# Tail scores in 64x64 quarters of TensorE, without zero padding, with a new order and new banks

## The chip, the cores and the metric

One core of a Trainium2 chip runs the whole kernel. The metric is the device time of one execution in microseconds: the median of three runs before the change is 801.45 us (800.21 to 803.18). The profiled execution took 798.73 us, of which 796.7 us lie between its first and its last instruction.

## The reference

Two stages follow one another, both in fp32. Stage 1 is attention with a threshold for 8 batches, 8 heads, 576 rows and 64 columns of a head; stage 2 is a mixture of 4 attention experts on its output, each row of which uses the two with the largest gate.

```python
# stage 1, for each batch and head: q, k, v are [576, 64]
scores = scale * q @ k.T
thresh = max(scores, -1) - tau
scores = where(scores >= thresh, scores, -1e9)
attn   = softmax(scores);  x = attn @ v           # x: [576, 512], all heads side by side
# stage 2, for each batch
logits = x @ w_gate;  topk = the two largest of 4;  w = softmax over these two
for e in range(4):
    q, k, v = x @ wq[e], x @ wk[e], x @ wv[e]     # [576, 64]
    a = softmax(where(causal, -1e9, scale * q @ k.T))
    out += (e in topk) * w[e] * (a @ v @ wo[e])
```

## The kernel before, in words

576 rows are four tiles of 128 rows and a tail of 64. Heads (stage 1) and experts (stage 2) are taken two at a time, since a head has 64 columns: one lies in partitions 0 to 63, the other in 64 to 127 (`heads` names the two halves). A full tile's scores of two heads are two matmuls of 64 rows by 128 columns that work in the upper and the lower half of the array, each into its own bank.

A tail has 64 rows only, so two of them make one tile of 128 output partitions. In stage 1 `scores` (line 942) joins the tails of two neighbouring pairs n-1 and n: `qz0` and `qz1` (line 807) are [128, 128] tiles of zeros in which `prep` fills the 64 columns of the one or the other pair. For each half of the columns (`hf`, 288 each) the kernel runs, for each head half j, the matmul of `qz0` with the keys of pair n-1 and adds that of `qz1` with those of pair n: eight matmuls of 64x128, of which half the columns multiply zeros. That is done once for each odd pair, 16 times. In stage 2 `scores2` (line 1143) joins the tails of the two experts of a pair `ep`: `q2d0` and `q2d1` (line 810) are block-diagonal tiles [128, 128], filled by two copies on ACT at the end of `projected` (line 1094); two matmuls over the full array use them, 16 times in all (8 batches, 2 pairs of experts).

Every fp32 matmul stands in the trace as two passes, each a LDWEIGHTS and a MATMUL row; those of projections and outputs (tiles in fp32r) are one pass.

The order is not written in the loops. Every operation is first put on a list with an estimate of its time. `arrange` (line 340) then sends the list through a model of the five engines: among the operations that are ready it takes the one with the lowest rank, a number from the tables `PLACE` and `PLACE_OP`; `CHANGE` (line 130) is what the model adds on TensorE when a matmul uses the array in another shape than the one before. `loosen` (line 487) gives every accumulation its bank from the table `BANKS`. `fill` (line 503) puts bf16 matmuls on a constant tile `still` where the model sees TensorE idle; there are 146. The engines then run their lists in that order, each waiting for semaphores.

A batch of stage 2 (`moe`) runs mixed with the next batch's stage 1. PE runs the scores, the transposes and the products; DVE reads scores out of the banks with their minimum (line 742, the mask at line 737); ACT runs two passes over each score tile (lines 760 and 754); POOL scales; SP starts DMAs, among them transposes of fp16 tiles (`T<-hl`).

Of the kernel before, what the change touches and what calls it, by code (L numbers as in the profile page):

```python
# [64 lines left out]
    "ctload": 21.58207, "ctt0": 0.8201564, "ctt1": 1.191231, "cvload": 0.7750551, "cvx": 0.7924649, "cvy": 0.2206414,  # L65
# [8 lines left out]
    "dtload": -2.15, "dtt0": 0.8163344, "dtt1": 0.9896782, "dvload": 51.9424, "dvx": 0.6755247, "dvy": 0.919954,  # L74
# [11 lines left out]
    "ovload": -7.436486, "ovx": 0.7431236, "ovy": 0.9078734, "perm": 3.2453, "qT": -0.2869131, "qload": 0.3382297,  # L86
# [4 lines left out]
}  # L91
PLACE_OP = {
    "ACT gw": -194.9887, "ACT kx": 131.3286, "ACT lg": 32.86921, "ACT p2": -202.4545, "ACT pb": -91.43077,
    "ACT pp": 101.5619, "ACT pt2": -21.09828, "ACT q2": 32.05941, "ACT q2d0": -14.54573, "ACT q2d1": -45.12697,
    "ACT qi": 86.16288, "ACT qx": -46.57733, "ACT qz0": -111.7469, "ACT qz1": -45.9329, "ACT tau_t": 9.119313,
    "ACT tq": -0.2682498, "ACT v2": 41.76934, "ACT warm": 50.16119, "ACT wkh": 33.61568, "ACT woh": -31.10502,
    "ACT wqh": -8.614884, "ACT wvh": -61.59402, "ACT x": -7.572205, "ACT z0": 69.30023, "ACT z1": 72.23125,
    "ACT zt": 70.11606, "DVE col": -77.59164, "DVE gate": -76.59955, "DVE gt": 21.13243, "DVE gw": -10.09983,
# [28 lines left out]
PSUMS = "s", "g"  # L127
LAST_OUT = 3
KEYS_BY = "DVE", "ACT"
CHANGE = ((0, 160, 195, 115, 110), (218, 23, 201, 119, 25), (198, 163, 0, 20, 120), (225, 165, 80, 0, 145), (216, 25, 223, 150, 50))  # L130
EXP_SB = True
AV2_GROUPS = ((4, 3), (2, 1, 0))
T2_GROUPS = ((4,), (3,), (2,), (1, 0))
# [424 lines left out]
def kernel(  # L558
# [249 lines left out]
    for t in qz:  # L808
        memset("POOL", t, 0.0)
# [515 lines left out]
```

## Time and profile before

| | |
|---|---|
| median of three runs | 801.45 us |
| profiled execution / its span | 798.73 us / 796.7 us |
| PE busy | 774.5 us, 97% |
| DVE busy | 697.1 us, 87% |
| ACT busy | 671.3 us, 84% |
| POOL busy | 390.9 us, 49% |
| stage-1 tail scores on PE (`kx,qz`) | 256 passes, 34.7 us busy |
| stage-2 tail scores on PE (`q,q2d`) | 64 passes, 19.6 us busy |
| ACT copies into `q2d` | 32, 6.8 us |

Busy time of PE runs to the modelled end of each matmul, and passes overlap; how long a group holds the array is therefore read from the starts of neighbouring groups in the timeline, not from busy time. A shape such as `64*128` is rows by columns of the array that the pass uses.

### The profile page before, as it was taken

What the parts mean: (1) busy time and instruction counts of PE and PEld (TensorE: products, weight loads), DVE (VectorE), ACT (ScalarE), POOL (GpSimd) and SP (SyncE); (2) the same over time, 40 slices, a digit from 0 to 9 for tenths busy, and PEclk for the clock granted to TensorE, in tenths of its full rate; (3) what the DMA queues carried; (4) which work ended last, traced back from release to release, by engine and by line L of the source; (5) the groups of instructions that cost most, each with busy time, mean ns of one, the idle gap of its engine ahead of it and who ended that gap; (6) DMA issues with size and microseconds to landing.
All of it is one profiled execution on the core that took longest, in us unless ns stands there. A gap on an engine that the chain in (4) does not pass through costs nothing.

```text
span 796.7 us, 27639 instructions
## 1 busy us (share of the span) xinstructions
PE 774.5 (97%) x10802; PEld 641.5 (81%) x10802; DVE 697.1 (87%) x2124; ACT 671.3 (84%) x1766; POOL 390.9 (49%) x551
## 2 busy tenths in 40 slices
PE   8999999999999999999999899999999999999998
PEld 6778878788878887788887787878877888778986
DVE  3999899988999899989899898998899988998374
ACT  4898789997999969998899878999799996998364
POOL 5774346643647336553365533664355733656010
PEclk9999999999999999999999999999999999999999
DMA  7431476856677668784759556695767755756102
GB/s 166 98 84 42 103 146 113 158 102 133 123 160 144 114 110 157 164 138 96 147 112 190 97 112 136 129 191 103 134 119 158 132 115 102 150 109 115 28 28 81
DMA packets 319010, 96.37 MB, mean 121 GB/s; under 512 B 305696, under 2 KB 314144, under 8 KB 318880
## 3 DMA queue, kind: packets, MB, share of 16 engines
q1 hardware_dynamic: 317152, 94.21, 59.7%
q8 instruction: 85, 1.39, 0.7%
q10 hardware_dynamic: 1728, 0.39, 0.3%
q14 instruction: 45, 0.37, 0.1%
HBM read 31.47 MB, written 9.44 MB: 51 GB/s over the span
## 4 chain that ended last, share of the span: by engine, by line
PE 61%; DVE 21%; ACT 9%; DMA 4%; issue 3%; POOL 0%; SPq 0%; POOLq 0%; ACTq 0%; DVEq 0%
PE banks L645 54%; DVE pp L742 7%; PE banks L1294 6%; DVE hl L731 5%; ACT pp L760 3%; ACT pp L754 2%; DVE p L737 2%; DMA T<-hl 2%; DVE col L708 2%; PE banks L1291 1%; DMA ki<-in_k_dram 1%; ACT p L754 1%; DVE pt L682 1%; DVE x L731 1%; ACT pt L680 1%
## 5 line engine op out<-in xcount | busy, mean ns | idle before, releaser
L760 ACT ACTIVATE pp<-pp,col 128x576 f32<-128x576 f32 x286 | 211.8, 774 | 25.7 <-DVE col L708 21.3
L742 DVE TENSOR_SCALAR_CACHE_REDUCE pp<-banks 128x576 f32<-128x576 f32 x286 | 207.4, 748 | 18.3 <-PE banks L645 14.4
L708 POOL TENSOR_SCALAR hl<-pp,col 128x576 f16<-128x576 f32 x182 | 148.1, 825 | 140.9 <-ACT q L680 25.0
L754 ACT ACTIVATE pp<-pp 128x576 f32<-128x576 f32 x286 | 193.7, 681 | 0.5
L731 DVE SCALAR_TENSOR_TENSOR hl<-pp,col,hl 128x576 f16<-128x576 f32 x182 | 172.8, 959 | 14.1 <-POOL hl L708 14.0
L645 PE MATMUL banks<-kx,qx 64*128 64x288 f32 x1024 | 158.4, 425 | 1.4 <-DVE pp L742 0.7
L708 POOL TENSOR_SCALAR pp<-pp,col 128x576 f32<-128x576 f32 x104 | 80.5, 785 | 79.6 <-DVE col L720 35.0
L645 PEld LDWEIGHTS banks<-kx,qx 64*128 64x128 f32 x1024 | 93.6, 189 | 29.8 <-issue 6.9
L708 POOL TENSOR_SCALAR p<-p,col,gw 128x384 f32<-128x384 f32 (+3 forms) x115 | 89.0, 782 | 45.7 <-ACT p L754 23.1
L754 ACT ACTIVATE p<-p,col 128x128 f32<-128x128 f32 (+4 forms) x137 | 78.8, 581 | 16.5 <-DVE col L737 14.8
L645 PE MATMUL banks<-T,vh 128*64 128x128 f16 (+1 forms) x2940 | 85.5, 216 | 3.0 <-DMA T<-hl 2.6
L645 PEld LDWEIGHTS <-vh 128*64 128x64 f16 x2940 | 79.6, 110 | 10.2 <-issue 8.8
L737 DVE CUSTOM_DVE_ANT_0 p<-banks,mask 128x128 f32<-128x128 f32 (+4 forms) x137 | 66.0, 503 | 4.3 <-PE banks L645 3.1
L645 PE MATMUL banks<-wvh,x 128*128 128x260 f32 x320 | 64.3, 288 | 0.0
L680 ACT ACTIVATE pt<-banks 128x384 f32<-128x384 f32 (+2 forms) x128 | 58.7, 506 | 1.8 <-DVE pp L742 1.1
L645 PEld LDWEIGHTS banks<-wvh,x 128*128 128x128 f32 x320 | 51.4, 188 | 6.8 <-issue 5.5
L754 ACT ACTIVATION_READ_ACCUMULATOR pp<-pp 128x1 f32 x286 | 56.4, 197 | 0.0
L645 PE MATMUL banks<-x,wkh 128*128 128x288 f32 x256 | 53.9, 303 | 0.8 <-DVE pp L742 0.8
L645 PE MATMUL banks<-q,q 64*128 64x256 f32 (+3 forms) x256 | 52.8, 463 | 1.9 <-ACT pt L680 0.8
L645 PE MATMUL banks<-x,wqh 128*128 128x288 f32 x256 | 52.0, 296 | 0.0
L645 PE MATMUL banks<-pt,v 128*64 128x128 f32 (+1 forms) x960 | 51.3, 259 | 0.0
L645 PEld LDWEIGHTS banks<-pt,v 128*64 128x64 f32 x960 | 43.6, 137 | 7.9 <-issue 4.6
(147 smaller groups left out, 1619.5 us busy)
## 6 DMA issues: line engine op xcount, KB each, us to landing
ki<-in_k_dram SPq DMA_DIRECT2D x32, 256.0 KB, 3.7
vz<-in_v_dram SPq DMA_DIRECT2D x32, 256.0 KB, 2.9
qi<-in_q_dram SPq DMA_DIRECT2D x62, 128.0 KB, 2.7
out_dram<-st SPq DMA_DIRECT2D x30, 256.0 KB, 2.5
tk<-in_k_dram SPq DMA_DIRECT2D x16, 128.0 KB, 3.9
T<-hl SPq DMA_TRANSPOSE x91, 4.8
vz<-in_v_dram SPq DMA_DIRECT2D x64, 16.0 KB, 2.5
out_dram<-st SPq DMA_DIRECT2D x8, 128.0 KB, 2.4
```

Source lines behind the costliest of these rows:

```text
L645: lambda o, x, y: nc.tensor.matmul(o, x, y, start=start, stop=stop))
L680: run(e, t, [dst], [src], lambda d, s: nc.scalar.activation(d, s, AF.Copy))
L682: run(e, t, [dst], [src], lambda d, s: nc.vector.tensor_copy(d, s))
L708: return m.tensor_scalar(d, s, x_, y_, op0=op0, op1=op1)
L731: return nc.vector.scalar_tensor_tensor(d, a_, x_, r.pop(0), op0=op0, op1=op1, **kw)
L737: lambda o, a, i, m: nc.vector.tensor_tensor_reduce(o, i, m, 1.0, 3e38, ALU.add, ALU.min, a))
L742: lambda o, a, i: nc.vector.tensor_scalar(o, i, 1.0, None, op0=ALU.mult, op1=ALU.min, accum_out=a))
L754: return nc.scalar.activation(d, s, AF.Exp, scale=scale, **kw)
L760: lambda d, s, x: nc.scalar.activation(d, s, AF.Prelu, bias=x, scale=-1.0, alpha=1e36))
L1291: nc.tensor.matmul(banks[:, n, :256], still_[:, :P], still_[:, :1].to_broadcast([P, 256]), start=True, stop=True)
L1294: o.fn(*(r.place() for r in (*o.outs, *o.ins)))
```

## The change

The tail scores use quarters of the array. In stage 1 `qz0` and `qz1` become [128, 64] tiles without zeros; each of the eight matmuls is 64x64 and writes into the half of the partitions that belongs to its pair, so nothing is added up. In stage 2 the `q2d` tiles and their copies are gone; for each half of the columns two 64x64 matmuls read the last 64 columns of the query tile itself, one in the upper left and one in the lower right quarter, both into one bank, in different partitions. The model gets a sixth shape. All numbers of `PLACE`, `PLACE_OP` and `BANKS` are new, so the order on every engine is.

```diff
-    "LMo0": 86.31751, "LMo1": 37.79194, "LMo2": 39.95239, "LMo3": 4.177216, "LMo4": 4, "La00": 80.50161,
+    "LMo0": 82.11209, "LMo1": 57.35111, "LMo2": 36.64272, "LMo3": 17.42819, "LMo4": 4, "La00": 75.58571,
...
-CHANGE = ((0, 160, 195, 115, 110), (218, 23, 201, 119, 25), (198, 163, 0, 20, 120), (225, 165, 80, 0, 145), (216, 25, 223, 150, 50))
+CHANGE = ((0, 160, 195, 115, 110, 160), (218, 23, 201, 119, 25, 150), (198, 163, 0, 20, 120, 163), (225, 165, 80, 0, 145, 165),
+          (216, 25, 223, 150, 50, 150), (218, 150, 201, 119, 150, 23))
...
-    def matmul(o, x, y, start, stop):
+    def matmul(o, x, y, start, stop, share=4):
...
         if form:
-            t /= 4 if form == 4 else 2
+            t /= share if form == 4 else 2
...
-        plan.ops[-1].mode = 4 if form and x.dtype in HALF else form
+        plan.ops[-1].mode = 4 if form and x.dtype in HALF else 5 if form == 4 else form
...
-    qz = [const(f"qz{i}", [P, P]) for i in range(2)]
-    for t in qz:
-        memset("POOL", t, 0.0)
-    q2ds = [const(f"q2d{i}", [P, P]) for i in range(2)]
+    qz = [const(f"qz{i}", [P, ST]) for i in range(2)]
...
-        for t in q2ds:
-            memset("POOL", t, 0.0)
...
-                outs.append((qz[n % 2][:, heads[n % 2]], gs[0][:, R * D:(R + 1) * D]))
+                outs.append((qz[n % 2], gs[0][:, R * D:(R + 1) * D]))
...
-                    matmul(sp[j][:, hf, :HS], x[rows], y[rows, o:o + HS], i == 0, i == len(qks) - 1)
+                    to = sp[j][:, hf, :HS] if len(qks) == 1 else sp[j][heads[i], hf, :HS]
+                    matmul(to, x[rows], y[rows, o:o + HS], True, True)
...
-                if i == 0 and hf:
-                    for j, sl in enumerate(heads):
-                        copy("ACT", q2ds[ep][sl, j * ST:(j + 1) * ST], g[sl, SM - HS:HS])
...
-                matmul(g[:, hf, :HS], q2ds[ep], q2[1][:, cols], True, True)
+                for rows in heads:
+                    matmul(g[rows, hf, :HS], q2[0][rows, SM:], q2[1][rows, cols], True, True, 2)
```

Three places on PE follow. The first is a stage-1 tail after scores of stage 2 (`q,q` are query and key tiles of the experts, `kx` keys, `col,ones` a small sum, `woh,z` the output). Before:

```order
L1294 MATMUL banks<-ident,p_77 128x64 x4
L645 MATMUL banks<-q_100,q_101 128x384 x2
L645 MATMUL banks<-q_100,q_101 128x512 x2
L645 MATMUL banks<-kx_65,qz_180 128x288 x2
L645 MATMUL banks<-kx_66,qz_181 128x288 x2
L645 MATMUL banks<-kx_65,qz_180 128x288 x2
L645 MATMUL banks<-kx_66,qz_181 128x288 x2
L645 MATMUL banks<-col_116,ones 64x1 x2
L645 MATMUL banks<-woh,z_106 128x512
```

The same place in the changed kernel:

```order
L1290 MATMUL banks<-ident,p_76 128x64 x4
L647 MATMUL banks<-q_101,q_100 128x384 x2
L647 MATMUL banks<-q_101,q_100 128x512 x2
L647 MATMUL banks<-kx_65,qz_180 64x288 x2
L647 MATMUL banks<-kx_66,qz_181 64x288 x2
L647 MATMUL banks<-kx_65,qz_180 64x288 x2
L647 MATMUL banks<-kx_66,qz_181 64x288 x2
L647 MATMUL banks<-col_155,ones 64x1 x2
L647 MATMUL banks<-woh,z_106 128x512
```

Nothing has moved here; the eight matmuls now stand in another shape than the scores before them. The second place is a stage-1 tail among stage 2's value and key projections (`wvh`, `wvl`, `wkh` with `x`). Before:

```order
L645 MATMUL banks<-wvl,x_93 128x260
L645 MATMUL banks<-wvh,x_94 128x260
L645 MATMUL banks<-kx_65,qz_180 128x288 x2
L645 MATMUL banks<-kx_66,qz_181 128x288 x2
L645 MATMUL banks<-kx_65,qz_180 128x288 x2
L645 MATMUL banks<-kx_66,qz_181 128x288 x2
L645 MATMUL banks<-wvh,x_95 128x260
```

In the changed kernel:

```order
L647 MATMUL banks<-wvl,x_93 128x260
L647 MATMUL banks<-wvh,x_94 128x260
L647 MATMUL banks<-kx_65,qz_180 64x288 x2
L647 MATMUL banks<-kx_66,qz_181 64x288 x2
L647 MATMUL banks<-kx_65,qz_180 64x288 x2
L647 MATMUL banks<-kx_66,qz_181 64x288 x2
L647 MATMUL banks<-x_95,wkh 128x288
```

The tail is again between full-array matmuls; a projection of keys follows it in place of one of values. The third place is the second stage-2 tail of a batch (`ident,qi` and `ident,tq` are transposes of queries, `T,vh` the fp16 products of stage 1). Before:

```order
L1294 MATMUL banks<-ident,p_77 128x64 x16
L1294 MATMUL banks<-ident,qi_62 128x64 x8
L1294 MATMUL banks<-ident,tq_88 128x64
L645 MATMUL banks<-q_100,q2d_183 128x288 x2
L645 MATMUL banks<-woh,z_106 128x512
L645 MATMUL banks<-wol,z_106 128x512
```

In the changed kernel:

```order
L1290 MATMUL banks<-ident,p_77 128x64 x16
L647 MATMUL banks<-kx_65,qx_63 128x288 x4
L647 MATMUL banks<-q_101,q_100 64x288 x4
L647 LDWEIGHTS vh_74
L647 MATMUL banks<-T_84,vh_74 64x64
```

The tail has left its place in front of the full-array output matmuls and stands between scores in halves of the array and fp16 products.

## Rows read from the trace of the kernel before

**Rows 1.** The page, part 1: busy time, share of the span, instructions.
```profile
PE 774.5 (97%) x10802; PEld 641.5 (81%) x10802; DVE 697.1 (87%) x2124; ACT 671.3 (84%) x1766; POOL 390.9 (49%) x551
```
**Rows 2.** Windows: us of each engine's busy time, granted clock, DMA share, GB/s.
```profile
100.00:200.00 100.00, 98.84 (x1421) 82.48 (x1422) 92.61 (x282) 89.52 (x240) 50.96 (x70) 1.00 0.68 130
...
400.00:500.00 100.00, 95.95 (x1358) 78.86 (x1353) 91.53 (x279) 87.30 (x231) 51.74 (x68) 1.00 0.66 126
500.00:600.00 100.00, 99.08 (x1368) 82.32 (x1367) 91.39 (x279) 89.87 (x237) 51.89 (x70) 1.00 0.71 138
...
sum 600.00, PE 586.40 PEld 485.01 DVE 551.54 ACT 532.15 POOL 305.41; mean PE 97.73 PEld 80.84 DVE 91.92 ACT 88.69 POOL 50.90
```
**Rows 3.** The page, part 4: chain that ended last, shares by engine.
```profile
PE 61%; DVE 21%; ACT 9%; DMA 4%; issue 3%; POOL 0%; SPq 0%; POOLq 0%; ACTq 0%; DVEq 0%
```
**Rows 4.** What PE waited for: us in total, times, longest us.
```profile
PE banks L645 <- DMA T<-hl: 2.6, 3, 1.4
PE banks L1294 <- DVE st L682: 2.6, 5, 0.6
PE banks L645 <- DVE pp L742: 2.1, 5, 0.6
```
**Rows 5.** Groups by form: busy us, mean ns | idle before, releasers.
```profile
L645 PE MATMUL banks<-kx,qz 64*128 64x288 f32 x256 | 34.7, 409 | 0.0
...
L645 PE MATMUL banks<-q,q2d 128*128 128x288 f32 x64 | 19.6, 429 | 0.0
...
L680 ACT ACTIVATE q2d<-banks 64x64 f32<-64x64 f32 x32 | 6.8, 212 | 2.5 <-PE banks L645 2.3
```
**Rows 6.** PE's timeline, a stage-1 tail, whole and in narrow windows: start, us, count.
```profile
24.32 2.21 PE L645 MATMUL banks<-kx,qz 64*128 64x288 f32 x16
...
24.67 0.65 PE L645 MATMUL banks<-kx,qz 64*128 64x288 f32 x4
...
24.91 0.65 PE L645 MATMUL banks<-kx,qz 64*128 64x288 f32 x4
...
26.36 1.14 PE L645 MATMUL banks<-kx,qx 64*128 64x288 f32 x8
```
**Rows 7.** PE's timeline, 106 to 113 us: scores in halves, a stage-2 tail.
```profile
106.69 1.14 PE L645 MATMUL banks<-kx,qx 64*128 64x288 f32 x8
107.76 1.87 PE L645 MATMUL banks<-T,vh 128*64 128x128 f16 x60
109.55 1.24 PE L645 MATMUL banks<-kx,qx 64*128 64x288 f32 x8
...
111.03 1.24 PE L645 MATMUL banks<-q,q2d 128*128 128x288 f32 x4
112.11 0.38 PE L1291 MATMUL banks<-still 128*128 128x256 bf16 x2
```
**Rows 8.** PE's timeline: scores in halves between projections.
```profile
126.45 1.24 PE L645 MATMUL banks<-kx,qx 64*128 64x288 f32 x8
127.63 0.53 PE L645 MATMUL banks<-x,wqh 128*128 128x288 f32 x2
128.00 0.29 PE L645 MATMUL banks<-x,wql 128*128 128x288 f32 x1
```
**Rows 9.** PE's timeline: scores in halves between transposes.
```profile
170.88 1.19 PE L645 MATMUL banks<-kx,qx 64*128 64x288 f32 x8
171.91 0.22 PE L1294 MATMUL banks<-ident,ki 64*128 64x64 f32 x1
```
**Rows 10.** PE's timeline: products in column halves.
```profile
176.81 1.07 PE L645 MATMUL banks<-pt,vz 128*64 128x128 f32 x16
177.72 0.39 PE L645 MATMUL banks<-pb,vz 128*64 128x128 f32 x4
```

More of the change, by code (lines that the diff above doesn't have):

```diff
@@ L35 @@
     "F0": 0.2926676, "F1": 0.6107417, "F2": 0.7488845, "F3": 0.7924216, "Fv0": 0.7107417, "Fv1": 0.8924216,
[29 rows of a table removed]
-    "ctload": 21.58207, "ctt0": 0.8201564, "ctt1": 1.191231, "cvload": 0.7750551, "cvx": 0.7924649, "cvy": 0.2206414,
[8 rows of a table removed]
-    "dtload": -2.15, "dtt0": 0.8163344, "dtt1": 0.9896782, "dvload": 51.9424, "dvx": 0.6755247, "dvy": 0.919954,
[11 rows of a table removed]
-    "ovload": -7.436486, "ovx": 0.7431236, "ovy": 0.9078734, "perm": 3.2453, "qT": -0.2869131, "qload": 0.3382297,
[4 rows of a table removed]
[29 rows of a table added]
+    "ctload": 21.58207, "ctt0": 0.7700778, "ctt1": 1.137123, "cvload": -74.82518, "cvx": 0.7517662, "cvy": 0.6509301,
[8 rows of a table added]
@@ L91 @@
+    "dtload": -2.15, "dtt0": 1.023116, "dtt1": 1.286915, "dvload": 54.26096, "dvx": 0.6755247, "dvy": 0.919954,
[11 rows of a table added]
+    "ott1": 1.277065, "ovload": -14.41097, "ovx": 0.7858482, "ovy": 1.264367, "perm": 3.2453, "qT": -0.09700796,
[5 rows of a table added]
 }
 PLACE_OP = {
-    "ACT gw": -194.9887, "ACT kx": 131.3286, "ACT lg": 32.86921, "ACT p2": -202.4545, "ACT pb": -91.43077,
-    "ACT pp": 101.5619, "ACT pt2": -21.09828, "ACT q2": 32.05941, "ACT q2d0": -14.54573, "ACT q2d1": -45.12697,
-    "ACT qi": 86.16288, "ACT qx": -46.57733, "ACT qz0": -111.7469, "ACT qz1": -45.9329, "ACT tau_t": 9.119313,
@@ L96 @@
-    "ACT tq": -0.2682498, "ACT v2": 41.76934, "ACT warm": 50.16119, "ACT wkh": 33.61568, "ACT woh": -31.10502,
-    "ACT wqh": -8.614884, "ACT wvh": -61.59402, "ACT x": -7.572205, "ACT z0": 69.30023, "ACT z1": 72.23125,
-    "ACT zt": 70.11606, "DVE col": -77.59164, "DVE gate": -76.59955, "DVE gt": 21.13243, "DVE gw": -10.09983,
-    "DVE hl": 160.1341, "DVE kx": -3.048238, "DVE lg": 91.45051, "DVE p2": -37.58712, "DVE pa": -19.18527,
-    "DVE pp": -37.24325, "DVE qsc": 87.14683, "DVE st": -16.99811, "DVE still": 70.0155, "DVE tau_p": -56.81983,
@@ L101 @@
-    "DVE v2": -191.0278, "DVE vh": 55.56019, "DVE warm": -33.54305, "DVE x": 12.58504, "DVE z0": 72.70677,
-    "DVE z1": 54.42244, "DVE zt": 99.32354, "POOL col": -52.95213, "POOL gate": 12.7582, "POOL gt": -10.22238,
-    "POOL gw": -13.52735, "POOL hl": 33.24148, "POOL ident": 56.04437, "POOL mask": 198.4146, "POOL mask2": -34.26997,
-    "POOL ones": -34.48011, "POOL p2": 35.40006, "POOL pp": 7.380059, "POOL q2d0": 57.69175, "POOL q2d1": -251.2611,
-    "POOL qz0": -8.171826, "POOL qz1": -64.26274, "POOL st": -36.63575, "POOL tie": -109.6021, "POOL v2": -16.65763,
@@ L106 @@
-    "POOL vh": -2.22825, "POOL vz0": 9.108861, "POOL vz1": -42.16982, "POOL wkh": -18.74004, "POOL wkl": -38.99,
-    "POOL woh": -8.639636, "POOL wol": 51.72843, "POOL wqh": 6.561986, "POOL wql": 38.53265, "POOL wvh": 13.17268,
-    "POOL wvl": -20.27672, "SP T": -176.0207, "SP ki": -46.37165, "SP lg": -43.14256, "SP out": -201.4397,
-    "SP qi": 35.10716, "SP st": -110.6428, "SP tk": -57.4548, "SP tq": -97.81713, "SP vz0": -79.04153,
-    "SP vz1": 30.91814,
+    "ACT gw": -194.1128, "ACT kx": 114.9448, "ACT lg": 32.86921, "ACT p2": -220.9327, "ACT pb": -131.8278,
@@ new lines @@
+    "ACT pp": 94.57432, "ACT pt2": -0.9630147, "ACT q2": -22.7764, "ACT q2d0": -19.04289, "ACT q2d1": -63.05565,
+    "ACT qi": 88.63102, "ACT qx": -74.94887, "ACT qz0": -72.21189, "ACT qz1": -38.38221, "ACT tau_t": 42.36084,
+    "ACT tq": 36.34548, "ACT v2": 46.58959, "ACT warm": 35.37198, "ACT wkh": 33.61568, "ACT woh": -31.10502,
+    "ACT wqh": -8.614884, "ACT wvh": -61.59402, "ACT x": 5.80622, "ACT z0": 74.16211, "ACT z1": 84.51968,
+    "ACT zt": 72.79803, "DVE col": -54.82467, "DVE gate": -72.99998, "DVE gt": 48.00172, "DVE gw": -35.83652,
@@ new lines @@
+    "DVE hl": 124.0373, "DVE kx": 42.31811, "DVE lg": 91.45051, "DVE p2": -24.25269, "DVE pa": 6.372014,
+    "DVE pp": -3.043822, "DVE qsc": 114.638, "DVE st": -33.50564, "DVE still": 9.346285, "DVE tau_p": -35.47929,
+    "DVE v2": -154.8319, "DVE vh": 41.7296, "DVE warm": -36.33248, "DVE x": 36.36639, "DVE z0": 25.83054,
+    "DVE z1": 57.76388, "DVE zt": 50.61126, "POOL col": -52.95213, "POOL gate": 10.24712, "POOL gt": -11.96009,
+    "POOL gw": -14.24344, "POOL hl": 27.21407, "POOL ident": 42.55757, "POOL mask": 190.1404, "POOL mask2": -88.54509,
@@ new lines @@
+    "POOL ones": -92.00483, "POOL p2": 14.29299, "POOL pp": -25.7627, "POOL q2d0": 82.12945, "POOL q2d1": -277.5747,
+    "POOL qz0": -58.87586, "POOL qz1": -44.37684, "POOL st": -13.22116, "POOL tie": -66.38262, "POOL v2": -23.868,
+    "POOL vh": -59.47183, "POOL vz0": -2.888774, "POOL vz1": -83.19861, "POOL wkh": -36.14122, "POOL wkl": -5.395328,
+    "POOL woh": 12.84353, "POOL wol": 93.3955, "POOL wqh": 32.64844, "POOL wql": 23.29405, "POOL wvh": 16.25282,
+    "POOL wvl": -58.56358, "SP T": -247.5121, "SP ki": -49.72211, "SP lg": -8.129818, "SP out": -198.0919,
@@ L111 @@
+    "SP qi": 4.023193, "SP st": -108.2689, "SP tk": -38.2543, "SP tq": -91.20736, "SP vz0": -12.86307,
+    "SP vz1": 2.693464,
 }
@@ L115 @@
 BANKS = (
-    "50310220464001102347610453234502462404620103272126767535237620164602344535401050134512060462050412563410432067"
-    "13250130277454102774376056461766744705431770770266562016642702040562602267543246906420653456503F0B2463120761N4"
-    "622648134045436216321143062730055601327077454206351742512565005670765140563070166205637D5311D07075062ND5130624"
-    "6627327E698044K2304324G4G4GH7366274730541034424045733072610322101445216507772400312020743154075456731605621511"
-    "461600727746583513062431277631B314251741645202E2E1C3J512326014106532112556706660423722755430740323304606505050"
-    "5416472265014370213064M1463C0665437BL950206244132424505720761712654003034QI26107032675270060527467043601320516"
-    "5542076240320140612215303301553167277055154830F35207611069C950206246332120G098606A703571020202489A764742610456"
-    "13245177400676502307623453572266731015332232104716055642370612175425042960661037B12B0206244723614C15D365177751"
-    "3612662B2L55710435471072263315270075H015440423214065571543110235540240462335406601232716120625L0763236B853150H"
-    "5210744145041353J110623054090F0902051073416735055765504674B5410242340557626732025E176740702313041305756572"
+    "5401400426246732013327362754100206266J264510251077521064675430363Q03630367046036762512522525355712570157754267"
+    "6504760140342513101766701257215026M710426044340455272650607306023646462423640240906420616544322I407513320653E7"
+    "48L4ED2C03413667151277653055347326762371415540560677306110423015604576313132130757253H2A0636404560350625020624"
+    "70322744250464L72650160AB4G3P90122025460612303632704164266732670055436636732307O244576000332543737007665267023"
+    "C027304015751C950206246023720527625531373210502202I95746235371023767147014374666532104205414711730125454237270"
+    "34063716151005721260A19052C207064145095030624175265403144102257456P1L54G151B2004605344051124073462763646325151"
+    "44501755466004C412120043064172512041765303405130I607207351D530F06245543033403F503032407620G4535703214667203562"
+    "110527502462766423010354507062046047D206516640744516414155060764302A603040550737603K030624015271714G41B1454273"
+    "1BC901I7A4267303727053410171420356376375431004323121436037104276411405306740145737021354068404602052768I520406"
+    "423754670C11D05C227451253255009401551533423163625103004175K24020131551364751766708562024761636024775643740"
 )
```

101 rows, old and new, of the table PLACE are left out of this document.

## Prediction

> **What bounds the kernel now.** I read the busy shares first, then the busy time in windows, the chain that ended last, what PE waited for, and last the timeline around the two tails. PE is busy for 97% of the span [rows 1]. In the 600 us in the middle the windows give PE 97.7 us of each 100, DVE 91.9 and ACT 88.7, at the full clock (2.4 GHz) [rows 2]. PE is on the chain for 61%, DVE for 21%, ACT for 9% [rows 3]. The waits that PE is seen in are small: the longest entries are 2.6 us in total each [rows 4]. So PE's own work sets the time, with DVE 6 points behind it; a saving on PE should reach the end until DVE takes over.
>
> **The stage-1 tail.** A tail is 16 passes in the trace. They run in pairs, one pass in each half of the array: two starts of a pair are 0.24 us apart (24.67, then 24.91), and 16 passes hold PE from 24.32 to 26.36, which is 2.04 us [rows 6]. The first step there is longer (24.32 to 24.67, 0.35 us), so a change of shape into fp32 work costs about 0.11 on top of eight steps of 0.242. That a pair costs one step is seen against the full array: the tail over 128x128 takes four passes from 111.03 to 112.11, 1.08 us, and eight half passes take 1.07 from 106.69 to 107.76 [rows 7]. Column halves pair in the same way: 16 passes of 128 columns take 0.91 us from 176.81 to 177.72, eight steps of 0.11 (each fp32 pass takes about 2 cycles for a column) [rows 10]. Quarters, in which rows and columns are both halved, don't occur before. The bounds are these: four at a time, as both kinds of halves together suggest, and the eight passes of each half of the columns take two steps in place of four, so a tail takes four steps in place of eight; or only two at a time, and nothing is gained. I take four at a time, since both kinds of halves run at full pace. 16 tails x 4 steps x 0.242 = 15.5 us less on PE (other bound: 0).
>
> **The stage-2 tail.** Two full-array matmuls (four passes, four steps) become four quarters (eight passes). If the upper left and the lower right quarter run together, that is again four steps and the term is 0. If they can't, it is eight steps, 16 x 4 x 0.242 = 15.5 us more. No row before has two row halves writing one bank: `kx,qx` pairs have a bank each. I take 0, by the nearest rows, the half-array pairs [rows 7].
>
> On that second bound two pages of the Trainium skill differ. "TensorEngine Tiling (Array Packing)", section Restrictions and Gotchas, says that different row tiles cannot access one PSUM bank at the same time; "PSUM — Partial Sum Buffer", section PSUM bank collisions raise a hardware error, reports collisions by bank and quadrant of partitions, and the two quarters write different partitions. By the first, taken as waiting, the sum would be 15.5 us worse; by the second nothing changes. No run here shows either yet; the first rule is part of the slower rival below.
>
> **The changes of shape.** A group pays when the array's shape differs from that of the group before. Four steps of half-array scores are 0.97 us. Between two full-array projections they take 126.45 to 127.63, 1.18 us: 0.11 to enter and 0.10 to leave; the first projection pass behind them is late too (0.37 from 127.63 to 128.00 for two passes, each 0.13, again 0.11 to enter) [rows 8]. Between transposes, which use 64x128 as well, they take 1.03 us: nearly nothing [rows 9]. Before fp16 products they pay the exit: 1.07 us with no entry [rows 7]. So a costly change is 0.10 for leaving and 0 to 0.11 for entering: 0.21 into two-pass or projection work, less into transposes and 128x64 work. I went down PE's order and counted neighbouring matmuls in different shapes: 487 before, 516 after. Without the two kinds that cost nothing (scores in halves to or from transposes, fp32 to or from fp16 in 128x64) it is 329 and 384. The quarters alone make 32 entries and 32 exits; a tail behind scores in halves paid nothing at entry and now does, and a stage-2 tail in front of output matmuls, both full array, paid nothing at exit and now does. 55 more at 0.17 (between 0.10 and 0.21, nearer to the upper end as most lead to or from fp32 work) = 9.4 us more; bounds 5.5 and 11.6.
>
> **ACT and the rest.** 32 copies into `q2d` go, 6.8 us of ACT [rows 5]. ACT has slack in every window, so only its share of the chain counts, 9% of 6.8 [rows 2, 3]: 0.6 us (bounds 0 and 6.8, the latter if every copy were on the path). The four memsets on POOL at the start are under DMA waits, and no work has taken their place: 0. The fillers are 146 in both orders: 0. DVE's and POOL's work stays the same.
>
> **The sum.** -15.5 + 0 + 9.4 - 0.6 = -6.7 us. Against the profiled execution's own 798.73 us (796.7 of span, 2.0 around it) that is 792.0; the median of the three runs is 2.7 above that execution, so I forecast 801.45 - 6.7 = 794.7.
>
> **What I can't see: the new order.** Every engine's list is laid out anew, so which semaphore comes late will differ. PE is idle for 13.6 us in the 600 us in the middle (600.00 - 586.40), between 0.9 and 4.1 in 100 [rows 2]. That is the size by which another order can be better or worse, by the same steps.
>
> **Rivals.**
> - The order also takes away waits. For it: a shorter tail on PE lets DVE start its two reads of the tile earlier, and the idle time varies fourfold between windows that run the same work, which an order could level. Against it: the windows are full already. Half of the 13.6 us gone gives 794.7 - 6.8 = 788.
> - DVE takes over, and PE's saving turns into waiting. For it: DVE is busy 91.9 of 100 us and 21% of the chain [rows 2, 3]; it frees the banks in which scores land. Against it: 6.7 us in 800 raise its share by less than one point. Time as before, 801 (797 to 806).
> - Quarters don't run side by side as halves do, in one of the two stages: either four at a time fail in stage 1, or the two of stage 2 wait for each other on their common bank. Either costs 15.5 us, and the order was laid out for the shorter time: 794.7 + 15.5 = 810. It decides as soon as a quarter group takes double its steps: a stage-1 tail over 1.9 us from its first pass to the next group, or a stage-2 tail over 1.9. For it: no row shows quarters, and the first page's rule. Against it: rows and columns each halve without loss.
> - A change that doesn't do what it says (no quarters at all) is seen in the order not to be so: the shapes stand there.
>
> **How the numbers follow.** Forecast 0.50, order better 0.17, DVE takes over 0.20, quarters wait 0.13. A difference of 0.5%, 4.0 us, is about what can be told from no change here: faster is below 797.4, slower above 805.5. The forecast's own range is 789 to 800 (switches at their bounds give 790.8 and 796.9, the rest is order); 0.44 of its 0.50 lie below 797.4 and 0.06 in between. Of the DVE case 0.17 lie within 0.5% and 0.03 above. Faster: 0.44 + 0.17 = 0.61; same: 0.06 + 0.17 = 0.23; slower: 0.03 + 0.13 = 0.16. The range 787 to 807 leaves out the slow rival and the lower half of the better order, 2 in 10.
>
> **What would show it.** Right: `kx,qz` passes as 64*64, a stage-1 tail of some 1.1 to 1.2 us from its first pass to the next group; a stage-2 tail of 1.1; PE's windows still at 97 to 98; ACT's busy time near 664. The switches are right if a group of scores between other shapes still takes 1.18. Wrong: tails of 2 us (quarters wait), or PE's idle time in the middle well over 14 us with DVE as the releaser (the saving became a wait), or well under it (the order gave more than the quarters).

## The result, and the profile after

The kernel after takes 776.46 us (median of four runs, 775.70 to 777.13), the kernel before 801.28 in the same rounds: a ratio of 0.9687, 95% interval 0.9667 to 0.9708. That is 24.8 us less, where 6.7 were forecast, and it lies below the range. The profiled execution took 776.71 (span 775.0).

The page after: busy shares, and the shares of the chain that ended last, to be read against [rows 1] and [rows 3].

```profile
PE 758.3 (98%) x10866; PEld 616.3 (80%) x10866; DVE 681.1 (88%) x2124; ACT 660.5 (85%) x1734; POOL 389.3 (50%) x547
...
PE 73%; DVE 13%; ACT 5%; DMA 5%; issue 3%; POOL 0%; SPq 0%; DVEq 0%; ACTq 0%; POOLq 0%
```

The windows after, 100 to 700 us in hundreds (the sum, against [rows 2]), and the first things that PE waited for ([rows 4]).

```profile
sum 600.00, PE 592.66 PEld 479.05 DVE 557.40 ACT 541.75 POOL 318.77; mean PE 98.78 PEld 79.84 DVE 92.90 ACT 90.29 POOL 53.13
```

```profile
PE banks L1290 <- DMA ki<-in_k_dram: 2.5, 3, 1.0
PE banks L1290 <- DVE pp L744: 2.0, 5, 0.7
PE banks L647 <- DMA T<-hl: 1.6, 3, 1.0
```

All engines are fuller, PE by one point. DVE's part of the chain has gone from 21% to 13%, ACT's from 9% to 5%. The tails run as forecast. PE's timeline after (start, us, engine, line, operation), a tail of stage 1 and one of stage 2:

```profile
181.29 1.20 PE L647 MATMUL banks<-kx,qz 64*64 64x288 f32 x16
182.42 0.40 PE L647 MATMUL banks<-x,wkh 128*128 128x288 f32 x1
...
291.81 1.19 PE L647 MATMUL banks<-q,q 64*64 64x288 f32 x8
292.92 0.50 PE L647 MATMUL banks<-woh,z 128*128 128x512 f32 x1
```

From its first pass to the next group a tail of stage 1 takes 1.13 us, with an entry and an exit in it, where it took 2.04 without an exit [rows 6]; one of stage 2 takes 1.11. The four passes of a stage-1 step start within some 20 ns of one another.

**An account of PE.** The busy row can't say where 24.8 us went: a pass is recorded with 0.4 us where the next follows after 0.12, so a short pause hides under the record. I therefore added up steps: every pass by its own step when nothing is late (a pair of half-height passes 0.242, four quarters 0.242, a full-height fp32r pass of 288 columns 0.133, and so on, read from undisturbed groups), then every costly change of shape (0.095 to leave, 0.02 to 0.10 to enter), and took the rest of the stretch from the first pass to the last as waiting. Waiting is so a remainder: an error in a step stands in every row alike, and differences are surer than sizes. In us, with the count of costly changes:

```
                                  passes   changes      waiting   stretch
before                            685.7    55.8 (329)   50.4      792.0
after                             670.2    63.9 (384)   36.2      770.2
pad12_in_new_order                685.7    62.2 (367)   38.5      786.4
pad1_in_new_order                 685.7    63.2 (376)   32.7      781.6
copies_in_new_order               670.2    63.9 (384)   38.1      772.1
q_in_old_order                    670.2    59.7 (357)   61.1      791.0
guard_q_in_old_order              670.2    59.7 (357)   52.1      782.0
own_banks_in_new_order            670.2    63.9 (384)   61.2      795.3
lru_banks_old_order               685.7    55.8 (329)   147.9     889.5
```

From before to after: passes -15.5, changes +8.1, waiting -14.2. The first two are the forecast's terms; the third had none. (The stretch falls by 21.8, the median by 24.8: before's profiled execution lay 2.6 below its median here.)

### The profile page after: what moved, and what is told of

Same layout as the page of the kernel before. It is cut to its first block, busy times and chain, and to the rows that moved or that the text cites. A ratio compares the mean times of both kernels' runs of the same rounds, so it can differ in the third digit from the quotient of the medians.

```text
span 775.0 us, 27724 instructions
## 1 busy us (share of the span) xinstructions
PE 758.3 (98%) x10866; PEld 616.3 (80%) x10866; DVE 681.1 (88%) x2124; ACT 660.5 (85%) x1734; POOL 389.3 (50%) x547
## 4 chain that ended last, share of the span: by engine, by line
PE 73%; DVE 13%; ACT 5%; DMA 5%; issue 3%; POOL 0%; SPq 0%; DVEq 0%; ACTq 0%; POOLq 0%
PE banks L647 64%; PE banks L1290 8%; DVE pp L744 4%; DMA T<-hl 2%; DVE hl L733 2%; DMA ki<-in_k_dram 2%; ACT pp L762 2%; ACT pp L756 2%; DVE col L710 1%; DVE p L739 1%; DVE pa L684 1%; PE banks L1287 1%; DVE st L684 1%; DMA tk<-in_k_dram 1%; ACT pt L682 1%
## 5 line engine op out<-in xcount | busy, mean ns | idle before, releaser
L762 ACT ACTIVATE pp<-pp,col 128x576 f32<-128x576 f32 x284 | 209.7, 772 | 18.0 <-DVE col L710 13.1
L710 POOL TENSOR_SCALAR hl<-pp,col 128x576 f16<-128x576 f32 x182 | 157.3, 876 | 131.0 <-ACT pp L762 34.5
L733 DVE SCALAR_TENSOR_TENSOR hl<-pp,col,hl 128x576 f16<-128x576 f32 x182 | 164.3, 911 | 4.5 <-POOL hl L710 4.5
L710 POOL TENSOR_SCALAR p<-p,col,gw 128x384 f32<-128x384 f32 (+3 forms) x116 | 84.2, 734 | 77.7 <-DVE col L722 46.6
L710 POOL TENSOR_SCALAR pp<-pp,col 128x576 f32<-128x576 f32 x102 | 78.2, 777 | 62.9 <-DVE col L722 28.0
L647 PEld LDWEIGHTS <-vh 128*64 128x64 f16 x2940 | 78.8, 110 | 11.9 <-issue 11.2
L756 ACT ACTIVATE p<-p,col 128x512 f32<-128x512 f32 (+4 forms) x135 | 78.7, 589 | 5.3 <-DVE col L739 4.7
L739 DVE CUSTOM_DVE_ANT_0 p<-banks,mask 128x512 f32<-128x512 f32 (+4 forms) x135 | 65.0, 515 | 6.4 <-PE banks L647 6.1
L647 PE MATMUL banks<-q,q 64*64 64x288 f32 (+4 forms) x384 | 65.2, 444 | 0.1
L682 ACT ACTIVATE pt<-banks 128x384 f32<-128x384 f32 (+2 forms) x128 | 57.0, 508 | 2.0 <-PE banks L1290 1.2
```

Of the source, the lines that this page charges most:

```text
L647: lambda o, x, y: nc.tensor.matmul(o, x, y, start=start, stop=stop))
L682: run(e, t, [dst], [src], lambda d, s: nc.scalar.activation(d, s, AF.Copy))
L710: return m.tensor_scalar(d, s, x_, y_, op0=op0, op1=op1)
L733: return nc.vector.scalar_tensor_tensor(d, a_, x_, r.pop(0), op0=op0, op1=op1, **kw)
L739: lambda o, a, i, m: nc.vector.tensor_tensor_reduce(o, i, m, 1.0, 3e38, ALU.add, ALU.min, a))
L756: return nc.scalar.activation(d, s, AF.Exp, scale=scale, **kw)
```

## The experiments

In each kernel the order of every engine's list is that of before or of after, as its name says, and only what is named is changed. Each time stands beside runs of before on the same chip; the ratio is to those.

### Quarters alone, order alone

```diff
 # q1_in_old_order: before, stage 1
+ plan.ops[-1].fn = lambda o, x, y, c=heads[i]: nc.tensor.matmul(o[c], x[:, c], y, start=True, stop=True)
 # q_in_old_order: and stage 2 (the copies into q2d stay)
+ plan.ops[-1].fn = lambda o, x, y: [nc.tensor.matmul(o[c], x[c, c], y[c], start=True, stop=True) for c in heads]
```

> The order of before, with quarters in the 16 stage-1 tails alone; stage 2 keeps its full-array tails. Theory O: 15.5 us of steps less, under 1 us more for shapes, 784 to 792 us, up to 3 us below the run with both stages in quarters. Theory Q: 772 to 778 us.

> The order, the banks and the fillers of before, unchanged on every engine; only what the 32 tails issue on PE differs: quarters in both stages (the copies into q2d stay and the quarters take its diagonal blocks). Theory O (the new order removed the waits, the quarters only work): PE saves 15.5 us of steps, pays some 3.4 us for shapes, and its waits stay at about 50 us: 786 to 794 us. Theory Q (the shorter tails themselves remove the waits): the waits fall by about 14 us here too, 774 to 779 us.

Measured: 797.53, ratio 0.9971 (0.9953 to 0.9988), with stage 1; 796.63, 0.9960 (0.9944 to 0.9976), with both. Both lie above the ranges of both theories. So the quarters of stage 2 by themselves are worth nothing that shows, and of the 15.5 us that stage 1's passes lose only 2 to 3 arrive. The chain of q_in_old_order, and what PE waits for first:

```profile
PE 44%; DVE 30%; ACT 14%; DMA 6%; issue 5%; POOL 1%; SPq 0%; DVEq 0%; POOLq 0%; ACTq 0%
```

```profile
PE banks L645 <- DVE pp L742: 6.2, 9, 1.4
```

PE's 61% of the chain [rows 3] became 44%, DVE's 21% became 30%, and the wait for the operation with which DVE empties score banks rose from 2.1 to 6.2 us [rows 4]. That is the forecast's second rival, in the old order.

```diff
 # pad1_in_new_order: after, stage 1 padded as before (qp: zeros but for one head)
+ plan.ops[-1].fn = lambda o, x, y, full=full, i=i, r=rows: nc.tensor.matmul(
+     full.place(), qp[i][r], y, start=i == 0, stop=i == 1)
...
 # pad12_in_new_order: stage 2 too, with its two ScalarE copies
+ nc.scalar.activation(q2ds[ep][sl, j * ST:(j + 1) * ST], s[sl, SM - HS:HS], AF.Copy)
...
+ plan.ops[-1].fn = (lambda o, x, y, full=full, ep=ep: nc.tensor.matmul(
+     full[0].place(), q2ds[ep], full[1].place(), start=True, stop=True)) if j else lambda *r: None
```

> The order, banks and fillers of the changed kernel, unchanged on every engine; the 16 stage-1 tails alone are issued as before, 64x128 with zeros. Theory O: the 15.5 us of steps come back and nothing else, 789 to 793 us. Theory Q: waits come back too, 798 to 806 us.

> The order of the changed kernel with the old tails in both stages (zeros in stage 1, full array and copies on ACT in stage 2): the new order by itself. Theory O: 15.5 us of steps more, 3 us less for shapes, 1 us for the copies: 787 to 793 us, so the order alone is worth 8 to 14 us. Theory Q: 800 to 806 us, the order alone is worth nothing.

Measured: 789.06, ratio 0.9863 (0.9841 to 0.9884), and 793.83, 0.9920 (0.9899 to 0.9941): in theory O's range, and 0.8 us above it. The order and its banks with the old tails are worth 6 us: 11.9 of waiting less, 6.4 of changes more. Neither half makes the 24.8. The halves are worth 0.4% and 0.8% alone and 3.1% together.

### What the old order loses to DVE

DVE's and POOL's timelines of before in one stretch (a wait before an operation in brackets):

```profile
184.03 2.98 DVE L731 SCALAR_TENSOR_TENSOR hl<-pp,col,hl 128x576 f16<-128x576 f32 x1 [0.94 <-POOL hl L708]
186.94 0.74 DVE L742 TENSOR_SCALAR_CACHE_REDUCE pp<-banks 128x576 f32<-128x576 f32 x1
```

```profile
183.94 0.31 POOL L687 MEMSET v<- 64x260 f32 x1
184.23 2.18 POOL L708 TENSOR_SCALAR hl<-pp,col 128x576 f16<-128x576 f32 x3
```

An operation whose median is 0.81 us takes 2.98 here. It begins 0.09 us behind a memset of POOL and 0.20 ahead of POOL's three `hl` operations and ends 0.60 after the last of them (186.41), so it has stood through all three. Before has six such places, one in each of six batches, 13 us in all; after has none (the longest is 1.37). Shorter holds, behind one scaling of POOL, are in both kernels: 30 of these operations took 1.0 to 1.3 us in before (14 us over the median), 40 took 1.0 to 1.4 in after (18 us). One such place in before, DVE's operation and the two of POOL beside it:

```profile
225.92 1.31 DVE L731 SCALAR_TENSOR_TENSOR hl<-pp,col,hl 128x576 f16<-128x576 f32 x1
```

```profile
225.89 0.74 POOL L708 TENSOR_SCALAR hl<-pp,col 128x576 f16<-128x576 f32 x1
226.61 1.24 POOL L708 TENSOR_SCALAR hl<-pp,col 128x576 f16<-128x576 f32 x1
```

Here too DVE ends 0.60 after the scaling that it stood behind (226.63), and the next scaling takes 0.50 longer. All 182 operations of this kind together, before and after (busy us, mean ns, then DVE's idle time before them):

```profile
L731 DVE SCALAR_TENSOR_TENSOR hl<-pp,col,hl 128x576 f16<-128x576 f32 x182 | 172.8, 959 | 14.1 <-POOL hl L708 14.0
L733 DVE SCALAR_TENSOR_TENSOR hl<-pp,col,hl 128x576 f16<-128x576 f32 x182 | 164.3, 911 | 4.5 <-POOL hl L710 4.5
```

In the new order this operation is shorter by 8.5 us in all, and DVE waits 9.5 us less for POOL ahead of it. To take away the six long holds I made POOL's string wait for DVE, by writing one column that DVE has just read:

```diff
+ if o.e == "POOL":
+     armed = o.outs[0].v.fams[0] == "v2" and not o.ins     # the memset ahead of the string
...
+ if armed and o.e == "DVE" and o.unit.endswith("h1") and o.outs[0].v.fams[0] == "hl":
+     nc.gpsimd.memset(o.ins[0].place()[:, :1], 0.0)
+     armed = False
```

> The kernel before with six memsets of one column on POOL, one a batch, that make POOL wait there until DVE's subtraction into hl is done; in the trace of before that DVE instruction takes 2.98 us in six batches, since a memset and three scalings of POOL run without a gap beside it, and 0.8 us elsewhere. All else as before. Theory S (these holds of 2.1 us, 13 us of DVE's time, are what binds the old order): 788 to 794 us against 799.9 for before on this chip. Theory L (the old order as a whole is laid out for the longer tails): 797 to 801 us.

> The same six guards in the old order with quarters in both stages, which without them took 796.6 us. Theory S: DVE no longer holds PE there and the saving of the quarters comes through, 779 to 786 us. Theory L: 793 to 798 us.

The hold is gone there. The same operation in guard_in_old_order, on DVE, and POOL's string behind it:

```profile
184.90 0.82 DVE L731 SCALAR_TENSOR_TENSOR hl<-pp,col,hl 128x576 f16<-128x576 f32 x1 [0.94 <-POOL hl L708]
```

```profile
185.78 0.10 POOL L1299 MEMSET pp<- 128x1 f32 x1 [0.66 <-DVE hl L731]
185.85 2.19 POOL L708 TENSOR_SCALAR hl<-pp,col 128x576 f16<-128x576 f32 x3
```

Measured: with padded tails 798.15, ratio 0.9976 (0.9953 to 0.9998), some 2 us; with quarters 788.98, 0.9869 (0.9839 to 0.9900). The first is in theory L's range, the second between the two. Thirteen us of DVE are worth 2 while PE sets the time and 7 to 8 once the quarters have made PE's work shorter. By the account the quarters alone cost the old order 3.9 us in changes and 10.7 in waiting, and the guards take 9.0 of waiting away (61.1 to 52.1). So of the 12 us that the old order withheld from the quarters some 4 went into changes of shape, and of the other 8 the guards give 7 back, 2 of which they give without the quarters too.

To see whether DVE binds the kernel after, I gave it 14.5 us of reductions into a tile that nothing reads, spread over six batches:

```diff
+ if o.e == "DVE" and o.unit.endswith("h1") and o.base in left:
...
+ for _ in range(3):
+     nc.vector.tensor_reduce(least, rest, axis=AX.X, op=ALU.max, apply_absolute_value=True)
```

> The changed kernel with three DVE reductions over 640 columns (0.8 us each) added behind one subtraction into hl in each of six batches, 14.5 us of DVE's time that nobody waits for by data. Theory S (DVE's time at this place is paid by the whole kernel): 783 to 790 us. Rival (the new order is bound by PE and DVE has room there): 774 to 779 us.

Measured: 779.80, ratio 0.9754 (0.9717 to 0.9791), against after's 0.9687, between the two ranges: about 5 of 14.5 us come through. DVE has room in the new order, but not much.

### The copies of stage 2

```diff
 # copies_in_new_order: after, and again
+ nc.scalar.activation(q2ds[ep][sl, j * ST:(j + 1) * ST], s[sl, SM - HS:HS], AF.Copy)   # read by nothing
 # pad2_in_new_order: after, with stage 2 alone padded (copies and full-array tail)
```

> The kernel after, with ScalarE's 32 copies into q2d put back where they were (nothing reads them); the tails stay in quarters. Theory C (the 4.8 us between pad12 and pad1 in the new order are these copies, 32 of 0.22 us on ScalarE, which delay the copies of q2 behind them): 779 to 783. Theory T (the tail itself: two full-height half-paces instead of quarters, and what waits for it): 774 to 778, as after.

> The kernel after with only the tails of stage 2 padded as before (q2d copies with them), those of stage 1 in quarters. If the stages add up, 775 + 4.8, so 779 to 782, and the rest of the 19 us between after and pad12 (14) is stage 1's 15.5 us of passes given back nearly whole. If what stage 2 costs is hidden once TensorE has time to spare, 775 to 777.

Measured: 779.20, ratio 0.9743 (0.9715 to 0.9770), and 779.09, 0.9739 (0.9706 to 0.9772): theory C, and stages that add up. The copies alone cost as much as copies and padded tail together, so the tail is worth nothing and 32 copies of 0.21 us cost 4 to 5 us, most of their 6.9:

```profile
L1095 ACT ACTIVATE q2d<-banks 64x64 f32<-64x64 f32 x32 | 6.9, 214 | 0.2
```

ACT is 12% of that kernel's chain, 5% of after's, and DVE 21% against 13%. What the copies cost in the old order wasn't run. Which of ACT's later operations hands the delay on isn't shown.

With these the change comes apart in order, each step a ratio: order and banks with the old tails 0.9920; without the copies 0.9863; quarters in stage 1 0.9687. That is 6, 5 and 14 us of 801.

### The banks

An engine's order is one half of the layout; the other is which of the eight PSUM banks each of the 1096 tiles gets. First fit (the banks in the families' own order) and longest free, with the orders kept:

```diff
- for v, x in zip(tiles, BANKS):
...
-     v.slot = self.families[v.fams[0]][DIGITS.index(x)]
+ # own_banks: the slot that the planner itself found free first
+ # lru_banks: v.slot = min(fits, key=lambda s: (max(free[u] for u in s.units), sum(free[u] for u in s.units)))
```

> The changed kernel with its order on every engine, but each accumulation keeps the bank that the model gave it when it sent it off, in place of the table of banks. If the table is part of what removed the waits: over 779 us. If only the order counts: within 2 us of the changed kernel, 773 to 778 us.

> The kernel before with each accumulation in the bank that the model gave it first, in place of its table. If the old table was worth as much to the old order as the new one to the new (25 us): 818 to 828 us. If the old order waits for DVE and ACT anyway and the table is worth little there: 800 to 808 us.

> The kernel before, its order unchanged on every engine, its table of banks replaced by a rule: each accumulation takes the bank (or two banks) that the model has had free for longest. Theory B (slack of the banks decides, whatever the table): 788 to 796 us. Rival F (a table is fitted to its own order, and a rule does worse than it): 800 to 812 us.

> The old order with quarters in both stages and the same rule for banks; with the old table it took 796.6 us. Theory B: the quarters' saving comes through, 776 to 788 us. Rival F: 794 to 806 us.

> The changed kernel's order with the same rule for banks; with its table 775 us on this scale, with the banks that the model gives first 800 us. Theory B: 774 to 780 us, the table is no better than the rule. Rival F: 783 to 797 us.

Measured: first fit 800.45 in the new order, ratio 1.0018 (0.9997 to 1.0038), and 819.11 in the old, 1.0224 (1.0189 to 1.0259). Longest free 892.51, 1.1149 (1.1102 to 1.1196), in the old order; 892.54, 1.1160 (1.1110 to 1.1209), with quarters; 860.96, 1.0746 (1.0710 to 1.0781), in the new order. Both first-fit runs are in the range for a table that matters; all three of longest free lie far above every range. I had looked for a gain from longest free, since it gives each bank the most time between two tiles. It lost most. PE's waits in lru_banks_old_order, and a place with PE and DVE beside each other:

```profile
PE banks L642 <- DVE pp L739: 59.6, 71, 1.8
PE banks L1291 <- DVE pp L739: 12.6, 16, 1.1
```

```profile
203.25 0.28 PE L642 MATMUL banks<-wvh,x 128*128 128x260 f32 x1
205.30 0.39 PE L642 MATMUL banks<-wvh,x 128*128 128x260 f32 x1 [1.76 <-DVE pp L739]
```

```profile
200.91 2.98 DVE L728 SCALAR_TENSOR_TENSOR hl<-pp,col,hl 128x576 f16<-128x576 f32 x1 [0.94 <-POOL hl L705]
203.81 0.74 DVE L739 TENSOR_SCALAR_CACHE_REDUCE pp<-banks 128x576 f32<-128x576 f32 x1
204.49 0.07 DVE L739 DVE_READ_ACCUMULATOR pp<-banks 128x1 f32 x1
204.49 0.74 DVE L739 TENSOR_SCALAR_CACHE_REDUCE pp<-banks 128x576 f32<-128x576 f32 x1
```

The projection at 205.30 writes bank 5, and the read it waits for is of a score tile in banks 3 and 6: they share nothing. A score tile is a view of two banks with a stride, and the program's waits treat all that lies between the two as used. Matching the program's waits to the trace in order, 82 of PE's pauses in this run, 69.1 us together, are of this kind; in before they are 3 and 1.1 us, in after 4 and 0.8, in own_banks_in_new_order 23 and 18.1, most of the 25 us that first fit loses there. A rule that avoids them, and takes near pairs, then the longest free:

```diff
+ for b, (l, h, e) in last.items():
+     if b not in bs and e > v.span[0] - 500 and (lo < b < hi or any(l < x < h for x in bs)):
+         met += 1
+ k = (met, hi - lo, max(free[u] for u in s.units), sum(free[u] for u in s.units))   # the least k
```

> The order before, its tiles padded as before, every engine's order kept; only the PSUM banks come from a rule in place of the table: among the free slots first the one that lies across, or between, the fewest banks of other tiles' pairs, then the closest pair, then the bank longest free. Theory B (the +92 us of the longest-free rule come from pairs of far banks: in that program 117 of TensorE's waits on VectorE are for a tile that lies between the two banks of the pair VectorE reads, and shares no bank with it; with the table 29, with this rule 19): close to the table, 797 to 812, TensorE's waits for VectorE under 15 us in all. Rival L (longest-free itself is bad, as it takes banks in an order that the engines do not release them in): still above 850. Rival F (any rule that does not know the order's details loses what the first-fit rule lost): 815 to 825.

> The order after with its quarters, banks by the same rule (near pairs, then longest free). Its program has 18 waits for a pair's between-bank, the longest-free rule's 111, the table's 23. Theory B: near the table, 776 to 786. Rival L: above 840. Rival F: about the 800 of the first-fit rule, which would mean that the table of after holds some 24 us that no such rule finds.

> The order before, tails in quarters, VectorE's six long holds behind GpSimd removed (as in guard_q_in_old_order, 789.0), and banks by the same rule. If what is left between 789 and the 775 of after is that the old table of banks was laid out for the padded tails' times, this lies under 786. If it is the order of the work on TensorE and VectorE (theory O), it stays at 789 or rises with the less fitted banks, to 789 to 800.

Measured: 814.29, ratio 1.0183 (1.0135 to 1.0232); 798.52, 0.9986 (0.9969 to 1.0003); 805.55, 1.0075 (1.0051 to 1.0100). The first lies between theory B's range and rival F's, the second is rival F's, the third lies above both. In the old order 77 of longest free's 92 us are gone by the rule, so banks in between are what longest free loses by, as theory B has it. It does not hold for the tables: the rule ends 15 us over the table of before and 24 over that of after, and 15 pauses for banks between, 11.7 us, remain in the new order where the table leaves 0.8. What else the tables have isn't shown.

The last run answers what the order alone is worth over quarters and free DVE: from 1.0075 to 0.9986 with the rule's banks (7 us), from 0.9869 to after's 0.9687 with each order's own table (14 us). The copies, which the new order has not, are in both differences: 4 to 5 us of each, if they cost there what they cost in the new order with its table, which no run shows. Order and table both have a part; I can't divide the rest further.

## Why the prediction was wrong

- **The stage-1 tail (-15.5): right.** Passes fell by 15.5 in the account, four at a time at 0.242.
- **The stage-2 tail (0): right.** Eight quarter passes take 1.11 us, and pad2_in_new_order and copies_in_new_order are 0.1 us apart. The Trainium skill's "TensorEngine Tiling (Array Packing)", section Restrictions and Gotchas, keeps row tiles off a common bank; here two row halves with different partitions of one bank ran at full pace, so the fear of 15.5 us more, and the rival built on it, fall.
- **The changes of shape (+9.4): right in size, +8.1.** But 6.4 of them come with the order even where the tails stay padded, not with the quarters; in the old order the quarters alone cost 3.9.
- **ACT's copies (-0.6): mis-sized.** They are worth 4 to 5 us in the new order. ACT's share of the chain says what lies on the path as it is; with the copies put back that share rose from 5% to 12% and DVE's from 13% to 21%, so their delay is handed on, and the bound named there, 6.8, was nearer.
- **The new order (0): the step that failed.** It was put at nothing, and its rival at half of the 13.6 us for which the windows show PE idle. By the account PE waits 36.5 us in those same 600 us of before; two thirds of that hide under recorded passes. After it is 20.3. The size taken from the idle row was short by a factor of about 2.7, and so were the rival and the range. Over the whole stretch waiting falls by 14.2, where passes and changes together give 7.4, near the forecast's 6.1; 11.9 of the 14.2 come with the order and its banks while the tails are still padded. Which waits went with the new order is shown in part only: DVE's six long holds are among what made them.
- **DVE takes over (0.20): true in the old order, not in the new.** Quarters in the old order gave 797 to 798, PE down to 44% of the chain. The argument against it, that DVE's share would rise by less than a point, weighed busy time and not the waits for DVE. The forecast held DVE's work as fixed; in the new order the six long holds behind POOL are gone, though shorter ones remain (DVE busy 697.1 [rows 1], now 681.1), and after's chain has 13% of DVE.
- The forecast added up tail and order as if each stood alone. The quarters of stage 1 are worth 2 to 3 us in one order and 14 in the other.

## What to carry to other kernels

Where passes overlap in the trace, work out an engine's waiting from steps, not from its idle row, before bounding what a new order can give. A saving on the engine that sets the time arrives only as far as the next engine can follow, so price it together with the layout that lets it. When tiles span two PSUM banks as one strided view, look at which other tiles' banks lie between: a rule that seems kind to the banks cost 92 us here.

## What the runs showed of the hardware

- Four fp32 quarters, in all four corners of the array, cost one step of 0.242 us for 288 columns, as one pair of halves did. Entering quarters costs about 0.05 us, entering full-array fp32 work 0.10.
- The held DVE operation reads two tiles in SBUF. The Trainium skill's "SBUF — State Buffer", section SBUF: two separate sides, tells of a lock between these two engines which the first to begin keeps for its whole instruction while the other blocks; for a DVE operation with two inputs in SBUF it is against a POOL operation that reads SBUF. The rows at 225.92 agree: DVE began 0.03 us behind a scaling of POOL and ended late, and POOL's next scaling then took 1.24 in place of 0.74. The rows at 184.03 agree on the blocking, but there POOL kept DVE out for three operations, not one. By the records DVE began 0.09 us behind a memset, which reads nothing (183.94), and 0.20 ahead of the first scaling (184.23). Since it ends 0.60 us after POOL in both places, some 0.2 of its 0.81 us seem to pass before POOL can hold it (an estimate from these rows), so the two came within hundredths of a microsecond of each other. Why DVE wasn't let in between the three isn't shown.
